# Chunks 0 and 1: gelu as one ScalarE activation, both convolved ahead of the first joint

## The chip, the cores and the metric

One core of one Trainium2 chip. Times are microseconds of device time for the whole kernel; several runs are given, and one further execution was recorded by the hardware profiler. Engines are called as the profile calls them: PE (TensorE), PEld (its weight loads), DVE (VectorE), ACT (ScalarE), POOL (GpSimd), SP (SyncE, which here only issues DMAs).

## The reference

A small speech transducer head, forward and backward. `x` is 2 x 16000 x 256, two strided convolutions with gelu reduce it to 4000 time steps, and a joint with 8 label vectors is formed by tanh:

```python
h = _gelu(conv3(x, w1))[:, ::2, :]          # conv3: three taps, 256 -> 256 channels
f = _gelu(conv3(h, w2))[:, ::2, :]          # _gelu: the tanh approximation
fe = jnp.einsum("btd,de->bte", f, w_f)
ge = jnp.einsum("bud,de->bue", g, w_g)
j = jnp.tanh(fe[:, :, None, :] + ge[:, None, :, :])
out = jnp.einsum("btud,dv->btuv", j, w_o)
# returned: out and the gradients of x, w1, w2, g, w_f, w_g, w_o for a given grad_out
```

All tensors are bf16. The largest are `out` and `grad_out` (2 x 4000 x 8 x 256, 32.8 MB each) and `x` and its gradient (16.4 MB each).

## The kernel before

The 8016 columns of time (both batches, with a gap of 16) are cut into 16 chunks of 512 (`CW`); the last is shorter. Channels lie on partitions, in two halves (`KT`). For each chunk n the kernel goes through these steps, each a Python generator that yields after a unit of work:

- `load_x(n)` brings the four phases of x (every fourth row) transposed into SBUF, one tile `XC` each, from a pool of six. `load_got` and `load_go` bring `grad_out` transposed and straight. All these are DMAs on SP's queue.
- `conv_units(n)` is the first convolution: for each parity of h two halves of six matmuls (L313), ACT copies each out of PSUM (L316), and `gelu` turns them into h (`HT`) and the derivative (`G1`).
- `conv2_units(n)` is the second convolution (L348, L351), with the same gelu giving f (`FT`) and its derivative (`G2`). `fe_units(n)` multiplies by w_f (L372) and copies to `FE` (L374).
- `tanh(n, u)` forms the joint's tanh for label u (`JT`, L389).
- `joint_units(n, up)` does two labels: `gj` squares JT (`JSQ`, L610), multiplies grad_out by w_o transposed (L616) and forms the gradient `NGZ` (DVE, L620); `ngfe_acc` sums NGZ over the labels on POOL (`ACCN`, last into `NGFE`, L639); JT is turned to rows (`JR`; by TensorE in `jr_block` for chunk 0, by DMA in `load_jr` after); the output is formed (L683) and copied (`OUT`, L685); `gwo` accumulates w_o's gradient (L722).
- the backward half of chunk n-1 runs inside chunk n's joint: `d1_units`, `d5_units`, `row_units`, `gwf_units`, `gw2_units`, `ghr_units`, `e_units` (L573 and L586), the last with the rows of x (`XR`) that `load_xr` brings on POOL's queue.

`gelu` is built from Square, a fused add and multiply, Sigmoid and a product (the list `first`), then five DVE operations for the derivative (the list `second`). Chunk 0 does this in halves of 512 columns.

Order: before the chunk loop, a `chain` writes out chunk 0's start: 16 dummy matmuls (`warm`, L766), the small products with g, both convolutions of chunk 0 with all weight transposes between them (`transposed_units`, L797), further dummies, and fe. Then for each chunk `weave` takes a unit of the joint, and after a share of them (`ratio`) a unit of the `fill`, which holds the convolutions of chunk n+1 and the backward half of chunk n-1. Deferred gelu operations wait in two queues, `later` (two per unit) and `late` (one per unit, while `late_open` is set). The order in which an engine gets its instructions is settled afterwards by a scheduler, which goes by this written order and by when inputs are ready; `keep_in_program_order` ties an instruction behind the one written before it on the same engine.

Of the kernel before, what the change touches and what calls it, by code (L numbers as in the profile page):

```python
# [32 lines left out]
def kernel(  # L33
# [173 lines left out]
    def load_xr(n):  # L207
        pin = tc.keep_in_program_order
        load = lambda **kw: pin(nc.gpsimd.dma_start(**kw))
# [29 lines left out]
    def scratch(name, spare):  # L239
        if spare:  # L240
            return rowp.tile([P, 8, P], BF16, name="rows")[:].rearrange("p (k a) b -> p k (a b)", k=KT)
        return gel.tile([P, KT, CW], BF16, name=name)
# [20 lines left out]
    def gelu(xb, W, h, gp, off, kts=((0, KT),), spare=False):  # L263

        sq, s = scratch("g_sq", spare), scratch("g_s", spare)
        TT, TS, STT = nc.vector.tensor_tensor, nc.vector.tensor_scalar, nc.vector.scalar_tensor_tensor
        first, second = [], []
        for (k0, k1) in kts:
            sq_, s_, x_ = sq[:, k0:k1, :W], s[:, k0:k1, :W], xb[:, k0:k1, :W]
            h_, gp_ = h[:, k0:k1, off:off + W], gp[:, k0:k1, off:off + W]  # L270
            first += [
                partial(nc.scalar.activation, out=sq_, in_=x_, func=ACT.Square, scale=GELU_R),
                partial(STT, out=s_, in0=sq_, scalar=1.0, in1=x_, op0=ALU.add, op1=ALU.mult),
                partial(nc.scalar.activation, out=s_, in_=s_, func=ACT.Sigmoid, scale=GELU_A),
                partial(TT, out=h_, in0=s_, in1=x_, op=ALU.mult),
            ]
            second += [
                partial(TS, out=sq_, in0=sq_, scalar1=3.0 * GELU_A, scalar2=GELU_A, op0=ALU.mult, op1=ALU.add),
                partial(TS, out=x_, in0=s_, scalar1=-1.0, scalar2=1.0, op0=ALU.mult, op1=ALU.add),
                partial(TT, out=sq_, in0=sq_, in1=x_, op=ALU.mult),  # L280
                partial(TT, out=sq_, in0=sq_, in1=h_, op=ALU.mult),
                partial(TT, out=gp_, in0=sq_, in1=s_, op=ALU.add),
            ]
        return first, second


    HALVES = ((0, 1), (1, 2))

    seconds0 = []

    def conv_units(n):
# [13 lines left out]
        taps = {0: ((1, 0, 0), (2, 1, 0), (0, 3, -1)), 1: ((0, 1, 0), (2, 3, 0), (1, 2, 0))}  # L305
        for par in range(2):
            xb = gel.tile([P, KT, CW], BF16, name="g_x")
            for mt in range(KT):
# [7 lines left out]
                nc.scalar.copy(out=xb[:, mt, :W], in_=ps[:, :W])  # L316
                yield
            first, second = gelu(xb, W, HT[:, par], G1[:, par], 2, HALVES if n == 0 else ((0, KT),))
            if par == 1 and n > 1:
# [4 lines left out]
            if n == 0:  # L324
                pump(len(first))
        seconds0.extend(seconds)
        if n > 0:
            seconds0.append(lambda: nc.gpsimd.tensor_copy(out=G1[:, 1, :, 1:2],
                                                          in_=S[n - 1]["G1"][:, 1, :, CW + 1:CW + 2]))

    def conv2_units(n):
# [3 lines left out]
        if n > 0:  # L335
            pump(len(later))
# [5 lines left out]
        xb = scratch("g_x", n == 0)  # L342
        for mt in range(KT):
# [7 lines left out]
            nc.scalar.copy(out=xb[:, mt, :W], in_=ps[:, :W])  # L351
            yield
        first, second = gelu(xb, W, FT, G2, 0, HALVES if n == 0 else ((0, KT),), n == 0)
        if n == 0:
            for f in first:
                f()
        else:
            later.extend(first)
# [4 lines left out]
    def fe_units(n):  # L363
        c0, W = geom(n)
        if n > 0:
            pump(len(later))
# [258 lines left out]
    def ngfe_acc(n, u):  # L625
# [13 lines left out]
        nc.gpsimd.tensor_tensor(out=out, in0=in0, in1=st["NGZ", u][:, :, :W], op=ALU.add)  # L639
# [18 lines left out]
    def jr_block(n, up, k):  # L658
        o, M = blocks(geom(n)[1])[k]
        srcs = [(S[n]["JT", 2 * up + j][:, kt, o:o + M], 2 * j + kt, M) for j in range(2) for kt in range(KT)]  # L660
        transposes(srcs, [(S[n]["JR", up][:M, :, :, k].rearrange("p u k d -> p (u k) d"), M, 0, 4)])

    def joint_units(n, up):
# [93 lines left out]
    nc.vector.memset(idle[:], 0.0)  # L757
    small = const.tile([P, 1], FP32, name="small")
    nc.vector.memset(small[:], 0.0)
    nc.scalar.activation(out=small[:], in_=small[:], func=ACT.Sigmoid)  # L760

    def warm(k):

        ps = ps_f32()
        for _ in range(k):
            tc.keep_in_program_order(nc.tensor.matmul(ps[:], lhsT=idle[:, 0, 0:P], rhs=idle[:, 0, 0:CW],  # L766
# [48 lines left out]
    load_jr(0, 0)  # L815

    for n in range(G):
        back, fwd = n > 0, n + 1 < G
        conv = conv_units(n + 1) if fwd else iter(())
        conv2 = conv2_units(n + 1) if fwd else iter(())  # L820
        late_open[0] = False
# [9 lines left out]
        else:  # L831
            parts += [conv, empty(3), islice(conv2, 1), empty(3), conv2, empty(3), fe_units(n + 1)]
        fill = chain(*parts)
        ratio = (0.92 if n > 0 else 0.4) if n + 1 < G else 0.72
        for up in range(U // 2):
# [8 lines left out]
            if up == 1:  # L844
                load_fr(n)
            main = joint_units(n, up)
# [92 lines left out]
```

## Time and profile before

| | us |
|---|---|
| median of 3 runs | 850.12 (849.65 to 863.76) |
| profiled execution | 860.22 |
| its span in the trace | 858.4 |
| PE busy in the span | 816.7 (95%) |
| ACT busy | 678.2 (79%) |
| DVE busy | 621.1 (72%) |
| POOL busy | 372.1 (43%) |
| granted TensorE clock, mean | 0.992 |

How to read it: the busy times are of the whole span. Lines of the profile name a line of the kernel, the engine, the operation and the tiles written and read; in the chain and the timeline the first number is the start in us from the span's start, the second the duration in us, and a bracket behind tells the idle time before and what ended it. Of a group of several instructions in one row (x20) the second number covers all of them. In the windows each row is a stretch of time, with the busy us of each engine, the granted clock, the DMA engines' share and GB/s.

### The profile page before, as it was taken

The numbers are of one execution on the slowest core, as the hardware profiler recorded it, in microseconds if no ns is written. First come the engines' busy times: TensorE is split into PE (matmuls) and PEld (weight loads), VectorE is DVE, ScalarE is ACT, GpSimd is POOL, SyncE is SP. The second block draws the span as 40 slices with busy tenths as digits, with TensorE's granted clock in tenths as the row PEclk, the third lists the DMA queues.
The fourth block names the chain that finished last, engine by engine and source line by source line (L and its number), as shares of the span: only waits on it lengthen the run. The fifth ranks groups of instructions, "written<-read, shape, count | busy, mean of one in ns | idle before, by whom it ended". The sixth has DMA issues, their size and how long they took to land.

```text
span 858.4 us, 16990 instructions
## 1 busy us (share of the span) xinstructions
PE 816.7 (95%) x6396; PEld 598.8 (70%) x6396; DVE 621.1 (72%) x1217; ACT 678.2 (79%) x1080; POOL 372.1 (43%) x367
## 2 busy tenths in 40 slices
PE   6979999999999999899999889999998899999997
PEld 2555676767668676677767667676685676868786
DVE  2997596776869677596876758768696666867745
ACT  2798998796979969699796787969799497896744
POOL 2144453344435434444565534444344243544661
PEclk8999999999999999999999999999999999999999
DMA  9986989999999999999999999999999999998965
GB/s 216 192 191 176 184 207 241 211 250 231 228 211 242 249 209 232 234 232 212 224 209 211 220 226 229 271 199 292 219 235 138 215 267 247 190 267 158 253 167 135
DMA packets 395474, 187.20 MB, mean 218 GB/s; under 512 B 345450, under 2 KB 381186, under 8 KB 393478
## 3 DMA queue, kind: packets, MB, share of 16 engines
q1 hardware_dynamic: 378112, 119.00, 77.5%
q0 software_dynamic: 17280, 67.12, 25.7%
q8 instruction: 50, 0.82, 0.4%
q14 instruction: 32, 0.26, 0.1%
HBM read 51.38 MB, written 50.34 MB: 119 GB/s over the span
## 4 chain that ended last, share of the span: by engine, by line
ACT 42%; PE 37%; DMA 9%; issue 5%; DVE 5%; POOL 0%; SPq 0%; ACTq 0%; POOLq 0%
ACT JT L389 13%; DMA JR<-JT 8%; ACT OUT L685 7%; ACT JSQ L610 6%; PE ps L586 6%; PE GWO_ps L722 5%; PE ps L573 5%; ACT rows L455 4%; PE ps L683 4%; PE ps L348 4%; PE ps L517 4%; PE ps L616 3%; ACT g_s L253 3%; ACT GX L576 3%; ACT g_x L316 2%
## 5 line engine op out<-in xcount | busy, mean ns | idle before, releaser
L639 POOL TENSOR_TENSOR ACCN<-ACCN,NGZ 128x1024 f32<-128x1024 f32 (+1 forms) x80 | 168.7, 2109 | 78.6 <-DVE NGZ L620 76.1
L620 DVE SCALAR_TENSOR_TENSOR NGZ<-JSQ,ps 128x512 bf16<-128x512 bf16 (+3 forms) x272 | 167.4, 640 | 46.2 <-PE ps L616 44.6
L685 ACT CAST OUT<-ps 128x512 bf16<-128x512 f32 (+1 forms) x252 | 148.7, 601 | 62.0 <-PE ps L683 61.8
L389 ACT ACTIVATE JT<-FE,GE 128x512 bf16<-128x512 f32 (+3 forms) x272 | 182.4, 713 | 9.5 <-DMA JR<-JT 9.0
L722 PE MATMUL GWO_ps<-GO,JR 128*128 128x256 bf16 (+1 forms) x1008 | 149.9, 273 | 11.0 <-DMA JR<-JT 8.8
L610 ACT ACTIVATE JSQ<-JT 128x1024 bf16<-128x1024 bf16 (+1 forms) x128 | 136.1, 1067 | 25.7 <-DVE NGZ L620 25.7
L683 PE MATMUL ps<-WO,JT 128*128 128x256 bf16 (+1 forms) x1008 | 148.5, 273 | 0.1
L616 PE MATMUL ps<-GOT,WOT 128*128 128x512 bf16 (+1 forms) x512 | 138.3, 374 | 3.2 <-ACT OUT L685 1.6
L710 POOL DMA_DIRECT2D out_dram<-OUT x76 | 55.9, 736 | 194.5 <-ACT OUT L685 182.8
L722 PEld LDWEIGHTS <-JR 128*128 128x128 bf16 (+1 forms) x1008 | 96.6, 98 | 40.1 <-DMA JR<-JT 10.7
L253 DVE SCALAR_TENSOR_TENSOR g_s<-g_sq,g_x 128x1024 bf16<-128x1024 bf16 (+2 forms) x49 | 82.3, 1680 | 54.4 <-ACT g_sq L253 54.4
L683 PEld LDWEIGHTS <-JT 128*128 128x128 bf16 (+1 forms) x1008 | 97.9, 98 | 21.9 <-issue 1.4
L573 PE MATMUL ps<-W1T,GH 128*128 128x256 bf16 (+2 forms) x756 | 100.5, 273 | 0.0
L401 DVE TENSOR_TENSOR ACC<-ACC,ps 128x512 f32<-128x512 f32 x90 | 61.5, 684 | 51.0 <-PE ps L517 35.0
L313 PE MATMUL ps<-XC,W 128*128 128x512 bf16 (+1 forms) x384 | 93.4, 381 | 4.1 <-DMA XC<-in_x_dram 4.1
L573 PEld LDWEIGHTS <-GH 128*128 128x128 bf16 (+2 forms) x756 | 83.4, 116 | 13.0
L586 PE MATMUL ps<-rows,XR 128*128 128x256 bf16 (+1 forms) x756 | 91.6, 275 | 0.0
L576 ACT CAST GX<-ps 128x512 bf16<-128x512 f32 (+2 forms) x126 | 72.3, 587 | 14.3 <-PE ps L573 8.2
L586 PEld LDWEIGHTS <-XR 128*128 128x128 bf16 (+1 forms) x756 | 74.6, 99 | 12.3
L234 POOL DMA_DIRECT2D out_dram<-GX x67 | 37.3, 558 | 88.0 <-ACT GX L576 83.1
L616 PEld LDWEIGHTS <-WOT 128*128 128x128 bf16 x512 | 48.3, 98 | 35.5 <-issue 3.9
L313 PEld LDWEIGHTS <-W 128*128 128x128 bf16 x384 | 37.9, 99 | 43.1 <-issue 7.2
(131 smaller groups left out, 1188.5 us busy)
## 6 DMA issues: line engine op xcount, KB each, us to landing
GO<-in_grad_out_dram SPq DMA_DIRECT2D x56, 512.0 KB, 5.5
out_dram<-OUT POOLq DMA_DIRECT2D x56, 512.0 KB, 5.4
XR<-in_x_dram POOLq DMA_DIRECT2D x13, 1088.0 KB, 8.6
out_dram<-GX POOLq DMA_DIRECT2D x55, 256.0 KB, 4.3
GOT<-in_grad_out_dram SPq DMA_TRANSPOSE x136, 5.3
JR<-JT SPq DMA_TRANSPOSE x128, 4.7
GO<-in_grad_out_dram SPq DMA_DIRECT2D x4, 384.0 KB, 4.0
out_dram<-OUT POOLq DMA_DIRECT2D x4, 384.0 KB, 4.7
```

What stands on the lines that cost most here:

```text
L253: later.popleft()()
L313: nc.tensor.matmul(ps[:, :W], lhsT=W1[:, i, kt, mt * P:(mt + 1) * P], rhs=st["X", c][:, kt, 16 + sh:16 + sh + W], start=(k == 0), stop=(k ...
L389: nc.scalar.activation(out=JT[:, mt, lo:hi], in_=S[n]["FE"][:, mt, lo:hi], func=ACT.Tanh, bias=GE[:, b, mt, u:u + 1], scale=1.0)
L573: nc.tensor.matmul(ps[:M, cj * D:(cj + 1) * D], lhsT=GH[:, par, kt, o:o + s * (M - 1) + 1:s], rhs=W1T[:, i, kt, :], start=(j == 0), stop=( ...
L586: nc.tensor.matmul(ps[:, dt * D:(dt + 1) * D], lhsT=XR[:M, 4 * k + i + 2 * (1 - par), dt * P:(dt + 1) * P], rhs=t[:M, g + 2 * par:g + 2 * ...
L610: nc.scalar.activation(out=JSQ[:, :, :W], in_=JT[:, :, :W], func=ACT.Square)
L616: nc.tensor.matmul(ps[:, :W], lhsT=WOT[:, kt, mt * P:(mt + 1) * P], rhs=GOT[:, kt, :W], start=(kt == 0), stop=(kt == KT - 1))
L620: nc.vector.scalar_tensor_tensor(out=NGZ[:, mt, lo:hi], in0=JSQ[:, mt, lo:hi], scalar=1.0, in1=ps[:, lo:hi], op0=ALU.subtract, op1=ALU.mul ...
L639: nc.gpsimd.tensor_tensor(out=out, in0=in0, in1=st["NGZ", u][:, :, :W], op=ALU.add)
L683: nc.tensor.matmul(ps[:M, j * V:(j + 1) * V], lhsT=st["JT", u][:, kt, o:o + M], rhs=WO[:, kt, :], start=(kt == 0), stop=(kt == KT - 1))
L685: nc.scalar.copy(out=OUT[:M, k, :], in_=ps[:M, :])
L722: nc.tensor.matmul(GWO_ps[:, dt, :], lhsT=JR[:M, j, dt, k, :], rhs=GO[:M, k, j * V:(j + 1) * V], start=(n_gwo[0] == 0), stop=(n_gwo[0] == ...
```

## The change

For chunks 0 and 1 ACT's `Gelu_apprx_tanh` reads PSUM and writes HT or FT at once; a DVE copy keeps the convolution's result for the derivative in a tile borrowed from the pools of GH (`XS`) or GF. The derivative recomputes Square, the inner term and Sigmoid from that copy, and its eight operations go into lists `deriv[n]` that are put into `late` at the start of chunk n's joint (opened in its third pass for chunk 0, from the beginning for chunk 1). Chunk 1's first convolution stands in the opening chain, two of its units ahead of chunk 0's second convolution; its second convolution follows the first tanh. Eight of nine weight transposes move into chunk 0's joint. Two of the three sets of dummies are dropped. x of chunk 1 is loaded ahead of grad_out; WO, W2 and WF load on POOL's queue; the x rows of chunk 0 are tied behind the last accumulation of chunk 0's joint. JR of chunk 0 is evicted for two blocks at a time.

```diff
-    def load_x(n):
+    def load_x(n, phases=(0, 1, 3, 2)):
-        for c in (1, 0, 3, 2):
+        for c in phases:
...
     def load_xr(n):
-        pin = tc.keep_in_program_order
-        load = lambda **kw: pin(nc.gpsimd.dma_start(**kw))
+        def load(**kw):
+            dma = tc.keep_in_program_order(nc.gpsimd.dma_start(**kw))
+            if n == 0:
+                tc.add_manual_dep(dma.ins, S[0]["last"].ins.name, NOSYNC, reason="x rows behind the joint")
...
+    def derivative(xb, W, h_, gp_):
+        TT, TS, STT = nc.vector.tensor_tensor, nc.vector.tensor_scalar, nc.vector.scalar_tensor_tensor
+        x_, t = xb[:, :, :W], {}
+        def square():
+            t["sq"] = gel.tile([P, KT, CW], BF16, name="g_sq")[:, :, :W]
+            nc.scalar.activation(out=t["sq"], in_=x_, func=ACT.Square, scale=GELU_R)
+        def inner():
+            t["s"] = gel.tile([P, KT, CW], BF16, name="g_s")[:, :, :W]
+            STT(out=t["s"], in0=t["sq"], scalar=1.0, in1=x_, op0=ALU.add, op1=ALU.mult)
+        return [
+            square,
+            inner,
+            lambda: nc.scalar.activation(out=t["s"], in_=t["s"], func=ACT.Sigmoid, scale=GELU_A),
+            lambda: TS(out=t["sq"], in0=t["sq"], scalar1=3.0 * GELU_A, scalar2=GELU_A, op0=ALU.mult, op1=ALU.add),
+            lambda: TS(out=x_, in0=t["s"], scalar1=-1.0, scalar2=1.0, op0=ALU.mult, op1=ALU.add),
+            lambda: TT(out=t["sq"], in0=t["sq"], in1=x_, op=ALU.mult),
+            lambda: TT(out=t["sq"], in0=t["sq"], in1=h_, op=ALU.mult),
+            lambda: TT(out=gp_, in0=t["sq"], in1=t["s"], op=ALU.add),
+        ]
+    deriv = {0: [], 1: []}
...
     def conv_units(n):
+        XS = ghp.tile([P, 2, KT, CW + 4], BF16, name="GH") if n <= 1 else None
-            xb = gel.tile([P, KT, CW], BF16, name="g_x")
+            xb = gel.tile([P, KT, CW], BF16, name="g_x") if n > 1 else XS[:, par]
...
-                nc.scalar.copy(out=xb[:, mt, :W], in_=ps[:, :W])
+                if n <= 1:
+                    nc.scalar.activation(out=HT[:, par, mt, 2:2 + W], in_=ps[:, :W], func=ACT.Gelu_apprx_tanh)
+                    nc.vector.tensor_copy(out=xb[:, mt, :W], in_=ps[:, :W])
+                else:
+                    nc.scalar.copy(out=xb[:, mt, :W], in_=ps[:, :W])
                 yield
+            if n <= 1:
+                deriv[n] += derivative(xb, W, HT[:, par, :, 2:2 + W], G1[:, par, :, 2:2 + W])
+                continue
...
     def conv2_units(n):
-        xb = scratch("g_x", n == 0)
+        xb = gfp.tile([P, KT, CW + 4], BF16, name="GF") if n <= 1 else scratch("g_x")
...
+            if n <= 1:
+                nc.scalar.activation(out=FT[:, mt, :W], in_=ps[:, :W], func=ACT.Gelu_apprx_tanh)
+                nc.vector.tensor_copy(out=xb[:, mt, :W], in_=ps[:, :W])
...
+        if n <= 1:
+            deriv[n][:0] = derivative(xb, W, FT[:, :, :W], G2[:, :, :W])
+            return
...
-        nc.gpsimd.tensor_tensor(out=out, in0=in0, in1=st["NGZ", u][:, :, :W], op=ALU.add)
+        st["last"] = nc.gpsimd.tensor_tensor(out=out, in0=in0, in1=st["NGZ", u][:, :, :W], op=ALU.add)
...
-            for k in range(len(bl)):
-                jr_block(n, up, k)
+            for k in (0, 2):
+                jr_blocks(n, up, k)          # eight transposes, one copy of 1024 columns
...
-    nc.sync.dma_start(out=W2[:], in_=w2.rearrange("i (kt p) n -> p i kt n", p=P))
-    nc.sync.dma_start(out=WF[:], in_=w_f.rearrange("(kt p) n -> p kt n", p=P))
-    nc.sync.dma_start(out=WO[:], in_=w_o.rearrange("(kt p) n -> p kt n", p=P))
-    idle = xcp.tile([P, KT, CW + 16], BF16, name="XC")
+    nc.gpsimd.dma_start(out=WO[:], in_=w_o.rearrange("(kt p) n -> p kt n", p=P))
+    nc.gpsimd.dma_start(out=W2[:], in_=w2.rearrange("i (kt p) n -> p i kt n", p=P))
+    nc.gpsimd.dma_start(out=WF[:], in_=w_f.rearrange("(kt p) n -> p kt n", p=P))
+    idle = rowp.tile([P, 8, P], BF16, name="rows")[:].rearrange("p a b -> p (a b)")
...
-    nc.scalar.activation(out=small[:], in_=small[:], func=ACT.Sigmoid)
+    nc.scalar.activation(out=small[:], in_=small[:], func=ACT.Gelu_apprx_tanh)
...
+    load_x(1, (0, 1, 3))
     for i in range(2):
         load_got(*order[i])
+    load_x(1, (2,))
     load_go(*orderp[0])
     for i in range(2, 4):
         load_got(*order[i])
-    if G > 1:
-        load_x(1)
-    for _ in chain(warm(16), small_units(), conv_units(0), transposed_units(), warm(8), conv2_units(0), warm(20), fe_units(0)):
+    conv1, turned = conv_units(1), transposed_units()
+    for _ in chain(warm(16), small_units(), conv_units(0), islice(turned, 1), islice(conv1, 2), conv2_units(0),
+                   conv1, fe_units(0)):
         pass
...
     load_jr(0, 0)
+    for _ in conv2_units(1):
+        pass
...
-        late_open[0] = False
+        late_open[0] = n == 1
+        if n <= 1:
+            late.extend(deriv[n])
...
-            parts += [conv, empty(3), islice(conv2, 1), empty(3), conv2, empty(3), fe_units(n + 1)]
+            parts += [turned, empty(12), fe_units(1)]
...
+            if n == 0 and up == 2:
+                late_open[0] = True
```

More of the change, by code (lines that the diff above doesn't have):

```diff
@@ L261, in pinned, with gelu @@
         return op if n <= 1 else (lambda: tc.keep_in_program_order(op()))
-    def gelu(xb, W, h, gp, off, kts=((0, KT),), spare=False):
-        sq, s = scratch("g_sq", spare), scratch("g_s", spare)
+    def gelu(xb, W, h, gp, off):
+        sq_, s_, x_ = scratch("g_sq")[:, :, :W], scratch("g_s")[:, :, :W], xb[:, :, :W]
+        h_, gp_ = h[:, :, off:off + W], gp[:, :, off:off + W]
         TT, TS, STT = nc.vector.tensor_tensor, nc.vector.tensor_scalar, nc.vector.scalar_tensor_tensor
[L267 to L283, printed above, removed]
-        return first, second
@@ L287 @@
-    HALVES = ((0, 1), (1, 2))
+        first = [
+            partial(nc.scalar.activation, out=sq_, in_=x_, func=ACT.Square, scale=GELU_R),
+            partial(STT, out=s_, in0=sq_, scalar=1.0, in1=x_, op0=ALU.add, op1=ALU.mult),
+            partial(nc.scalar.activation, out=s_, in_=s_, func=ACT.Sigmoid, scale=GELU_A),
+            partial(TT, out=h_, in0=s_, in1=x_, op=ALU.mult),
+        ]
+        second = [
+            partial(TS, out=sq_, in0=sq_, scalar1=3.0 * GELU_A, scalar2=GELU_A, op0=ALU.mult, op1=ALU.add),
+            partial(TS, out=x_, in0=s_, scalar1=-1.0, scalar2=1.0, op0=ALU.mult, op1=ALU.add),
+            partial(TT, out=sq_, in0=sq_, in1=x_, op=ALU.mult),
+            partial(TT, out=sq_, in0=sq_, in1=h_, op=ALU.mult),
+            partial(TT, out=gp_, in0=sq_, in1=s_, op=ALU.add),
+        ]
@@ L350, in conv2_units @@
                     k += 1
-            nc.scalar.copy(out=xb[:, mt, :W], in_=ps[:, :W])
-            yield
[L353 to L358, printed above, removed]
+            if n <= 1:
+                nc.scalar.activation(out=FT[:, mt, :W], in_=ps[:, :W], func=ACT.Gelu_apprx_tanh)
+                nc.vector.tensor_copy(out=xb[:, mt, :W], in_=ps[:, :W])
+            else:
+                nc.scalar.copy(out=xb[:, mt, :W], in_=ps[:, :W])
+            yield
+        if n <= 1:
+            deriv[n][:0] = derivative(xb, W, FT[:, :, :W], G2[:, :, :W])
+            return
+        first, second = gelu(xb, W, FT, G2, 0)
+        later.extend(first)
         late.extend(pinned(f, n) for f in second + seconds0)
@@ L364, in fe_units @@
         c0, W = geom(n)
-        if n > 0:
-            pump(len(later))
+        pump(len(later))
         FE = fep.tile([P, KT, CW], FP32, name="FE")
```

36 lines of the change are left out of this document (18 added, 18 removed).

## The prediction

> **What bounds the kernel now.** I read the page's slices first (PE 8 to 9 tenths nearly everywhere, 6 and 7 in the first and third), then the windows, which put numbers on that.
>
> ```profile
> core 0: us, PE busy (x) PEld busy (x) DVE busy (x) ACT busy (x) POOL busy (x), PEclk, DMA share, GB/s
> 33.00:77.00 44.00, 37.64 (x264) 23.31 (x263) 37.89 (x79) 40.08 (x62) 19.11 (x13) 0.96 0.79 175
> 77.00:127.00 50.00, 49.29 (x391) 36.53 (x390) 39.09 (x70) 45.84 (x73) 21.06 (x20) 1.00 0.92 200
> 127.00:177.00 50.00, 49.33 (x392) 36.69 (x391) 37.57 (x69) 41.64 (x66) 22.17 (x20) 1.00 1.10 233
> ```
>
> From 77 us on TensorE is busy 49.3 of 50 us: nothing in the change touches those fourteen chunks, so only what precedes can be won. The accumulation's last step per chunk (POOL L639 writing NGFE) marks the chunks:
>
> ```profile
> 74.26 2.13 POOL L639 TENSOR_TENSOR NGFE<-ACCN,NGZ 128x1024 bf16<-128x1024 f32 x1
> 122.97 2.45 POOL L639 TENSOR_TENSOR NGFE<-ACCN,NGZ 128x1024 bf16<-128x1024 f32 x1 [1.03 <-DVE NGZ L620]
> 173.75 2.45 POOL L639 TENSOR_TENSOR NGFE<-ACCN,NGZ 128x1024 bf16<-128x1024 f32 x1 [1.03 <-DVE NGZ L620]
> ```
>
> So 76.4 us pass until chunk 0's joint is summed; then a chunk takes 50.8. The sum is about these 76.4 us. Their chain:
>
> ```profile
> 3.49 10.62 DMA XC<-in_x_dram
> 14.16 3.59 PE ps L313 x8
> ...
> 23.91 1.89 PE ps L766 x8
> 25.80 2.61 PE ps L348 x12
> 28.40 4.32 PE ps L766 x20
> 33.19 1.07 ACT FE L374 x2
> 34.26 2.45 ACT JT L389 x4
> ...
> 37.69 2.52 DVE NGZ L620 x8
> ```
>
> A load of x until 14.1 us, the first convolution, then a stretch in which the chain passes through 28 dummy matmuls (L766), which only fill the time the gelu steps of chunk 0 take. The first NGZ stands at 37.7. From the timeline:
>
> ```profile
> 0.74 1.28 ACT L760 ACT_TABLE_LOAD   x1 [0.74 <-PEq L923]
> 4.77 1.07 POOL L209 DMA_DIRECT2D XR<-in_x_dram  x2
> 14.16 6.61 PE L313 MATMUL ps<-XC,W 128*128 128x512 bf16 x20 [4.08 <-DMA XC<-in_x_dram]
> 17.21 0.29 DVE L258 TENSOR_SCALAR g_sq<-g_sq 128x512 bf16<-128x512 bf16 x1
> 45.35 0.43 DVE L258 TENSOR_SCALAR g_x<-g_s 128x1024 bf16<-128x1024 bf16 x1
> 53.94 2.35 DVE L258 TENSOR_SCALAR g_x<-g_s 128x1024 bf16<-128x1024 bf16 x1
> ```
>
> Two things to see. Twenty matmuls take 6.61 us where 12 take 2.61 later (0.217 each, so 4.3): the windows give a granted clock of 0.50 from 12 to 18 us, after the wait. And the written order is not the executed one: XR belongs to chunk 1's code and the derivative at 17.21 to chunk 0's joint, yet both run far ahead of it. The scheduler fills idle engines with whatever is ready.
>
> **The change, step by step.**
>
> *Loading x.* XR (1,080 KB by the issue view) leaves the first 14 us; WO, W2 and WF (640 KB) take its place on POOL's queue, from SP's, where they stood behind x. SP loses three issues (0.58, 0.53, 4.82), gains x of chunk 1 ahead of GOT and GO. The third x part landed at 14.1 together with about 1.6 MB of POOL's queue since 2.3 (0.135 MB per us) against 0.79 MB of x. At those rates the new 1.19 MB of POOL end at 11.1 with 0.58 MB of x in; the last 0.2 MB at the 0.2 MB/us of later windows take 1 us: 12.1 us. Bounds: 10.3 us (all 1.97 MB at the windows' rates) and 14.1 (if the transposes set their own pace). TensorE then waits 2 us instead of 4.08; of the 2.3 us lost to the clock I save 1.3 (bounds 0 and 2.3). The convolution ends at about 17.4 instead of 20.8.
>
> *Convolving chunk 1 ahead.* Between that end and FE's first copy lie 12.4 us now. Then: four transposes 0.2, and 12+12+12+4 matmuls by 0.217, 8.7. These hide the gelu steps, as the dummies did. x of chunk 1 has two free buffers out of six; its third part waits in SP's queue until chunk 0's first half is convolved (about 15), and lands 4.2 later (median of L164), at 19 to 20, when TensorE arrives at 18.5: wait 1 us (bounds 0 and 4; behind it in SP's queue are GOT and GO, which now land some 12 us before use). FE's copy at about 27.3 instead of 33.2: **-5.9**.
>
> *Gelu in one step.* ACT's GELU reading PSUM is not in the trace. Nearest rows: CAST of the same shape from PSUM 0.58, tanh 0.71. I take 0.58, so it costs what the copy did, and Square, the fused step, Sigmoid and the product (0.63, 0.69, 0.63, 0.42 per half) go off the path. In exchange 12 copies PSUM to SBUF on DVE, 0.69 each by L443: 8.3 us, against the products saved, 6 x 0.42 and 3 x 0.69, 4.6. In the first 20 us DVE works 3.5, so it hides them; without that cover 3.7.
>
> *Tables.* Now one load serves Sigmoid and Tanh. GELU asks for a further one, and the first Sigmoid for a switch. The derivatives' six Sigmoids are written late, but may be pulled forward as L258 was; each one between two GELUs costs two loads, 2.56. Bounds: one load, hidden, and six pairs, 15.4. I take three pairs, 7.7 us, of which ACT's idle time (busy 4.8 of the first 20 us and 7 of the next 13, by the windows) hides all but **+2.2**, the two GELUs of chunk 1's second convolution ahead of JSQ among it. The rule that speaks against the change is here. "Batch activation calls by set, not by function", says the Trainium skill (ScalarE: Activation LUTs, "Table sets: the hidden batching unit"), and its "What ACT_TABLE_LOAD costs" gives an estimate of 2.66 us a switch with its drain; the row's 1.28 shows the load alone, no run here shows the drain, and by 2.66 the three pairs would be 16 us.
>
> The first NGZ follows FE by 4.5 us as now; the first joint's start moves from 37.7 to about 34: **-3.7**.
>
> *Chunk 0's joint* (37.7 to 76.4). It loses 36 matmuls of chunk 1 (7.8 us) and six copies on ACT (3.5), gets 32 weight transposes (1.7) with eight copies on DVE (2.7) and JR evictions in pairs (eight of 0.61 for sixteen of 0.34, by back-to-back starts). But ACT is busy 40 of 44 us and DVE 38, so TensorE's relief is worth nothing itself. What counts: ACT 3.5 less, and a wait that goes. Now fe of chunk 1 waits for FT in the middle of this joint, behind a stretched DVE operation (2.35 where the same took 0.43, under a POOL accumulation); TensorE's gaps of 2.13, 1.56 and 1.48 us and its halved clock (0.89 between 55 and 70) stem from there. With FT done before, I take **-4**. Bounds: +2 (three late derivatives of chunk 0 join those of chunk 1: ACT 5.8, DVE 11) and -11 (ACT's bare work with no derivative in it: tanh, JSQ and OUT of four passes, 6.3 each, and two GELUs or FE copies twice 1.2).
>
> *Chunk 1's joint.* Its derivatives are written into it: DVE 3 x (1.22+2x0.43+3x0.69), less some overlap at their ends, 11 to 12, ACT 3 x 1.92 = 5.8, beside 39 and 46 of 50. Since ready work is pulled ahead, I take **0**; left in place it is +2 to +5, as ACT would need 51.6 of 50 us. XR now comes on POOL's queue after the last accumulation, as in all other chunks; it lands in 8.6 us, some 20 before gw1 (L586) asks for it, and POOL's stores stand behind only its issue of 0.55.
>
> *Rest.* The idle tile and the buffers of GH and GF lent for x wait for no one before chunk 1; POOL's memsets of them no longer run at 5.8 but in POOL's free half. 0.
>
> Sum: -3.7 - 4 + 0 = **-7.7 us**. The profiled execution took 860.2 (span 858.4 and 1.8 around it), so 852.5 by its own time. Its spacing of NGFE shows gaps of 53.7, 53.9, 55.2 and 58.4 where others are 50.8, where the chain waits for JR transposes; the runs shown have a median 10 us lower. The median is the base of the forecast: 850.1 - 7.7 = **842.4**.
>
> **Rivals.**
>
> 1. *More is won.* No Sigmoid falls between GELUs (start -5.9), and the joint comes near ACT's bare work, -9: -15, **835**. For: in the first 33 us ACT is idle 21, room for all 11.6 us of Squares and Sigmoids. Against: DVE stretched by POOL stays.
>
> 2. *Slower: tables thrash.* All six Sigmoids stand alone among GELUs while TensorE waits for ACT: 15.4 us on the path. With -5.9 and -4 that is +5.5, and the half clock after each wait costs about 1.5 more: **857**. It decides from four pairs on the path (4 x 2.56 = 10.2 against 9.9). For: L258 at 17.21. Against: ACT has gaps in the start, and a late GELU of chunk 1 is not asked for at once. By the Trainium skill's 2.66 (same page, same section), as an estimate, it would be 873.
>
> 3. *Derivatives stay where written.* Chunk 1 becomes ACT's, +5: **847**. For: three scratch buffers for six sets of them. Against: L258 again.
>
> 4. *XR was not what held x.* The third part still lands at 14: 3.5 of the start come back, and the wait for chunk 1's third part grows by 0.4: **846.3**. For: the fourth transpose's issue already took 2.87 instead of 1.28, so SP's queue alone is backed up at 7 us. Against: XR ends at 14.3, with x. The Trainium skill (DMA: Bandwidth & Descriptors, "Queues, rings and completion order") says each engine goes round the queues packet by packet; by that x is held by whatever POOL has queued, weights as much as XR; with half of the step's 3.4 lost it would be 844, an estimate.
>
> **How the numbers follow.** Forecast 0.42, rivals 0.18, 0.12, 0.15, 0.13. The range runs from rival 1 and somewhat beyond, for stalls of JR that the median may hold fewer of, 831, to 853, short of rival 2. A measurement of this kernel can tell about 2%, 17 us: faster needs 833 or less, beyond rival 1's own value, so half of that and a little of the forecast, 0.13; slower needs 867, a part of rival 2 with the dearer switch, 0.05; the rest, 0.82, is within 2%.
>
> **What would show it.** Right: L313's wait on XC about 2 us and its end near 17; FE's first copy near 27; first NGZ near 34; NGFE of chunk 0 near 68.5 and the next 48.7 to 51 later; some seven ACT_TABLE_LOAD. Wrong: XC still landing at 14 (rival 4); a dozen loads and TensorE waiting for HT or FT (rival 2); NGFE 0 to NGFE 1 over 53 (rival 3); NGFE 0 before 62 (rival 1); or a difference that arises after chunk 2, which no step here has.

## Result and profile after

| | before | after |
|---|---|---|
| median, us (4 runs each) | 855.80 (849.65 to 863.76) | 879.76 (875.03 to 884.98) |
| ratio of after to before | | 1.0289, 95% interval 1.0226 to 1.0351 |
| profiled execution, its span, us | 860.22, 858.4 | 875.03, 873.3 |
| granted TensorE clock, mean | 0.992 | 0.979 |
| DVE busy, ACT busy, us | 621.1, 678.2 | 622.8, 679.4 |
| first NGZ, us | 37.7 | 45.5 |
| last accumulation of chunk 0 starts | 74.3 | 74.7 |
| last accumulation of chunk 1 starts | 123.0 | 136.2 |

The kernel became slower by some 24 us, where 7.7 us less had been forecast. No engine has more to do: DVE and ACT are busy for practically as long as before. A ratio leaves out runs more than 1.5% above their kernel's fastest, whereas medians are of all runs; in chunks from 2 on, waits for JR transposes come and go from run to run in both kernels, so profiles are compared only up to chunk 1's last accumulation.

The loss is there at that point already: the two profiled spans differ by 14.9 us, and 13.3 of it have arisen by then. First the rows of the last accumulation, from the timeline of POOL after:

```profile
74.66 3.00 POOL L666 TENSOR_TENSOR NGFE<-ACCN,NGZ 128x1024 bf16<-128x1024 f32 x1
136.22 2.45 POOL L666 TENSOR_TENSOR NGFE<-ACCN,NGZ 128x1024 bf16<-128x1024 f32 x1 [1.04 <-DVE NGZ L647]
187.23 2.45 POOL L666 TENSOR_TENSOR NGFE<-ACCN,NGZ 128x1024 bf16<-128x1024 f32 x1 [1.03 <-DVE NGZ L647]
```

From 74.66 to 136.22 chunk 1 takes 61.6 us; before, it took 48.7. The next chunk takes 51.0, against 50.8. So there are two things to explain: an opening that ends 7.8 us later although it was to be shorter, and a chunk 1 that is 12.9 us longer. Between them chunk 0's joint gains: from its first NGZ to the end of its last accumulation it takes 32.1 us (45.5 to 77.7) instead of 38.7.

**The opening.** The same stretch of the timeline as was shown of before, now after:

```profile
0.74 1.28 ACT L791 ACT_TABLE_LOAD   x1 [0.74 <-PEq L962]
10.16 1.87 PE L334 MATMUL ps<-XC,W 128*128 128x512 bf16 x4
12.94 6.46 PE L334 MATMUL ps<-XC,W 128*128 128x512 bf16 x20 [0.91 <-DMA XC<-in_x_dram]
13.98 0.60 ACT L338 ACTIVATE HT<-ps 128x512 bf16<-128x512 f32 x1 [11.75 <-PE ps L334]
14.62 0.69 DVE L339 CAST GH<-ps 128x512 bf16<-128x512 f32 x1 [4.10 <-ACT HT L338]
30.31 3.57 PE L334 MATMUL ps<-XC,W 128*128 128x512 bf16 x8 [9.82 <-DMA XC<-in_x_dram]
45.52 0.68 DVE L647 SCALAR_TENSOR_TENSOR NGZ<-JSQ,ps 128x512 bf16<-128x512 bf16 x1
58.90 1.28 ACT L300 ACT_TABLE_LOAD   x1
```

Chunk 0's convolution now waits only 0.91 us, and ends at 19.4. But then four matmuls of chunk 1's convolution run, and TensorE stands for 9.82 us: the third part of chunk 1's x isn't there until 30.3. The eight matmuls behind this wait take 3.57 us, 0.45 each, where 12 took 2.61 (0.22 each). SP's queue, from its timeline, shows why x is late:

```profile
0.75 13.35 SPq L164 DMA_TRANSPOSE XC<-in_x_dram  x6
14.14 2.65 SPq L172 DMA_TRANSPOSE GOT<-in_grad_out_dram  x2
16.83 0.58 SPq L198 DMA_DIRECT2D GO<-in_grad_out_dram  x1
17.47 5.57 SPq L172 DMA_TRANSPOSE GOT<-in_grad_out_dram  x3
23.09 1.13 SPq L198 DMA_DIRECT2D GO<-in_grad_out_dram  x2
24.33 9.10 SPq L164 DMA_TRANSPOSE XC<-in_x_dram  x5
```

The second column is the time in which the queue was busy issuing. The source has the third part of x ahead of every GOT and GO. In the queue five GOT and three GO stand ahead of it: it could not start until chunk 0's convolution had freed a buffer, the others could, and so the scheduler put them first. They took the queue from 14.1 to 24.2 us. When x had its buffer, it was behind them.

**Chunk 1.** The windows, first of before and then of after (us, then busy us of each engine, the granted clock, DMA share, GB/s):

```profile
60.00:78.00 18.00, 14.38 (x97) 9.03 (x95) 13.91 (x30) 15.14 (x24) 10.85 (x6) 0.91 0.53 147
78.00:90.00 12.00, 12.00 (x93) 7.77 (x91) 8.43 (x15) 11.53 (x18) 3.08 (x3) 1.00 1.05 200
90.00:102.00 12.00, 11.29 (x100) 8.55 (x98) 7.54 (x16) 12.00 (x19) 4.58 (x4) 1.00 0.81 188
102.00:114.00 12.00, 12.00 (x100) 9.51 (x98) 9.68 (x17) 8.34 (x14) 6.65 (x6) 1.00 0.91 196
```

```profile
core 0: us, PE busy (x) PEld busy (x) DVE busy (x) ACT busy (x) POOL busy (x), PEclk, DMA share, GB/s
60.00:78.00 18.00, 15.35 (x106) 10.37 (x104) 17.20 (x27) 15.54 (x24) 9.61 (x7) 0.91 0.81 184
78.00:90.00 12.00, 9.96 (x77) 6.39 (x76) 11.90 (x20) 10.82 (x16) 4.34 (x7) 1.00 0.95 219
90.00:102.00 12.00, 7.63 (x51) 4.06 (x48) 11.84 (x23) 11.54 (x16) 1.48 (x3) 1.00 1.20 242
102.00:114.00 12.00, 9.69 (x69) 7.31 (x70) 6.47 (x12) 7.28 (x12) 4.97 (x4) 0.72 0.45 93
```

From 60 to 102 us DVE is now busy 40.9 of 42 us (17.20 + 11.90 + 11.84); before, it was 29.9. ACT, the other engine that the derivatives use, is no busier than it was (37.9 us, before 38.7). So DVE is the bound there, and TensorE starves: from 78 to 114 it is idle 8.7 of 36 us where it was idle 0.7, and in the last of these stretches it has a clock of 0.72. That costs by estimate another 2.2 us (0.28 of 12, less half of the 2.3 us in which it stood idle there). Together (8.7 - 0.7 + 2.2) that is about 10.2 of the 12.9 us. What DVE does more of is the derivatives: their rows take 24.6 of its 40.9 us from 60 to 102; before, L258 took 4.2 of 29.9. Three rows of DVE, one of POOL, two of ACT and two of TensorE after:

```profile
61.39 2.25 DVE L302 TENSOR_SCALAR GF<-g_s 128x1024 bf16<-128x1024 bf16 x1
84.88 2.35 DVE L302 TENSOR_SCALAR GF<-g_s 128x1024 bf16<-128x1024 bf16 x1
114.80 0.68 DVE L305 TENSOR_TENSOR G<-g_sq,g_s 128x1024 bf16<-128x1024 bf16 x1
...
84.77 2.17 POOL L666 TENSOR_TENSOR ACCN<-NGZ 128x1024 f32<-128x1024 bf16 x1 [4.05 <-DVE NGZ L647]
...
95.49 1.07 ACT L300 ACTIVATE g_s<-g_s 128x1024 bf16<-128x1024 bf16 x1
96.44 2.56 ACT L416 ACTIVATE JT<-FE,GE 128x512 bf16<-128x512 f32 x4
...
87.88 0.38 PE L467 MATMUL ps<-GF,W2T 128*128 128x512 bf16 x1 [1.39 <-DVE GF L446]
104.31 0.61 PE L753 MATMUL GWO_ps<-GO,JR 128*128 128x256 bf16 x2 [4.97 <-DMA JR<-JT]
```

The derivative rows stretch from 61.4 to 115.5 us, three sets of chunk 0 up to 80 and three of chunk 1 from 82. An operation that takes 0.42 us alone takes 2.25 and 2.35 beside a POOL accumulation. TensorE's longest wait, 4.97 us, is for a transposed JR: ACT forms the JT for it at 96.4, right behind the Sigmoid of a derivative (95.5). Before, chunk 0's derivatives ran between 17 and 36 us, in the opening, where their 9.3 us of DVE fitted beside 8.1 of its other work. After, only a Square (38.0), a fused step (39.1) and one further operation (41.5) ran that early.

### The profile page after: what moved, and what is told of

Same layout as the page of the kernel before. It is cut to its first block, busy times and chain, and to the rows that moved or that the text cites. A ratio compares the mean times of both kernels' runs of the same rounds, so it can differ in the third digit from the quotient of the medians.

```text
span 873.3 us, 16905 instructions
## 1 busy us (share of the span) xinstructions
PE 819.4 (94%) x6368; PEld 599.0 (69%) x6368; DVE 622.8 (71%) x1194; ACT 679.4 (78%) x1075; POOL 374.4 (43%) x370
## 4 chain that ended last, share of the span: by engine, by line
ACT 41%; PE 36%; DMA 8%; DVE 6%; issue 6%; SPq 3%; POOL 0%; ACTq 0%; POOLq 0%
ACT JT L416 13%; ACT OUT L716 7%; ACT JSQ L637 6%; DMA JR<-JT 6%; PE ps L613 6%; PE GWO_ps L753 5%; PE ps L600 5%; PE ps L714 5%; PE ps L544 4%; ACT rows L482 4%; PE ps L373 4%; PE ps L643 3%; ACT g_s L254 3%; ACT GX L603 3%; ACT g_x L341 2%
## 5 line engine op out<-in xcount | busy, mean ns | idle before, releaser
L716 ACT CAST OUT<-ps 128x512 bf16<-128x512 f32 (+1 forms) x252 | 148.8, 601 | 62.7 <-PE ps L714 62.1
L637 ACT ACTIVATE JSQ<-JT 128x1024 bf16<-128x1024 bf16 (+1 forms) x128 | 135.8, 1067 | 24.2 <-DVE NGZ L647 24.2
L714 PE MATMUL ps<-WO,JT 128*128 128x256 bf16 (+1 forms) x1008 | 151.3, 275 | 2.4 <-ACT g_x L341 0.9
L753 PEld LDWEIGHTS <-JR 128*128 128x128 bf16 (+1 forms) x1008 | 97.3, 99 | 40.6 <-DMA JR<-JT 11.0
L254 DVE SCALAR_TENSOR_TENSOR g_s<-g_sq,g_x 128x1024 bf16<-128x1024 bf16 (+1 forms) x42 | 73.1, 1740 | 51.9 <-ACT g_sq L254 51.9
L334 PE MATMUL ps<-XC,W 128*128 128x512 bf16 (+1 forms) x384 | 95.6, 388 | 12.4 <-DMA XC<-in_x_dram 10.7
```

What stands on the lines that cost most here:

```text
L254: later.popleft()()
L334: nc.tensor.matmul(ps[:, :W], lhsT=W1[:, i, kt, mt * P:(mt + 1) * P], rhs=st["X", c][:, kt, 16 + sh:16 + sh + W], start=(k == 0), stop=(k ...
L637: nc.scalar.activation(out=JSQ[:, :, :W], in_=JT[:, :, :W], func=ACT.Square)
L714: nc.tensor.matmul(ps[:M, j * V:(j + 1) * V], lhsT=st["JT", u][:, kt, o:o + M], rhs=WO[:, kt, :], start=(kt == 0), stop=(kt == KT - 1))
L716: nc.scalar.copy(out=OUT[:M, k, :], in_=ps[:M, :])
L753: nc.tensor.matmul(GWO_ps[:, dt, :], lhsT=JR[:M, j, dt, k, :], rhs=GO[:M, k, j * V:(j + 1) * V], start=(n_gwo[0] == 0), stop=(n_gwo[0] == ...
```

## Experiments

My theory after the result: two faults that don't depend on each other, the late third part of x and the late derivatives. The rivals: that the gelu's own operations or the table loads are what costs; that the opening's loads only move the wait elsewhere; and that something lasting comes in behind chunk 2. "Lead" below is how much earlier than in the kernel before (123.0) chunk 1's last accumulation starts; a negative one is later.

**The kernel after once more** (no edit).

> The changed kernel once more, unaltered. Theory (the loss stands in two places before 139 us: TensorE's 9.8 us wait for the third x part of chunk 1, and the derivatives that fill DVE from 60 to 102 us): the last accumulation of chunks 0 and 1 starts again near 74.7 and 136.2 us, within 1 us, and the later chunks differ only by chance waits for JR transposes. Rival (a lasting change of the transposes' order on SP's queue): the last two chunks again take some 87 us from one last accumulation to the next but one, where the kernel before took 80.

877.69 us against 859.47, ratio 1.0207 (1.0138 to 1.0277). First NGZ 46.2, chunk 1 66.5 us, lead -18.3. The wait for x is 8.43 us. Both faults are there again, at sizes that vary by 1 to 5 us: chunk 0 came as expected, chunk 1 by 5 us later than expected. From 90 to 110 us TensorE waits 9.6 us for JR transposes in three waits, where after had the one of 4.97, and DVE is busy 37.0 of the 42 us from 60 to 102. So the share of JR in the second fault varies. The loss at chunk 1 (13.3 and 18.3) and in the total (24 and 18.2) are of similar size.

**Opening loads kept in their written order.**

```diff
 # load_got and load_go, while the opening is written
-            nc.sync.dma_start_transpose(out=t[:, :, col:col + w], in_=grad_out[b, q:q + w, u, :])
+            dma = nc.sync.dma_start_transpose(...)
+            if opening[0]:
+                tc.keep_in_program_order(dma)
```

> The loads of grad_out in the opening are tied to the written order on SP's queue, so the third x part of chunk 1 goes ahead of them. Theory: it lands near 20 us instead of 30.3, TensorE's wait shrinks from 9.8 to under 2 us, the first NGZ moves from 45.5 to about 36, the last accumulation of chunk 0 from 74.7 to about 66, and chunk 1 still takes 61: some 9 us faster than the changed kernel, 868 to 871. Rival (the bytes, not the order: 4.9 MB are asked for before the first joint, 24 us at 0.2 MB per us): the x part or the first GOT lands late all the same, chunk 0 ends at 72 or later, and the time stays within 3 us.

```profile
14.05 6.67 PE L340 MATMUL ps<-XC,W 128*128 128x512 bf16 x20 [2.95 <-DMA XC<-in_x_dram]
37.59 0.38 PE L834 MATMUL pst<-ident,W 128*128 128x128 bf16 x4 [0.21 <-ACT OUT L722]
49.36 1.89 PE L649 MATMUL ps<-GOT,WOT 128*128 128x512 bf16 x4 [2.32 <-DMA GOT<-in_grad_out_dram]
```

These are all the waits that TensorE's timeline marks between 12 and 60 us. The wait for the third part has gone; the first NGZ comes at 35.0 instead of 45.5 and chunk 0's accumulation at 65.0. A GOT comes 2.32 us late in exchange. The order of SP's queue was the cause of the late opening. The forecast had 34 for the first NGZ, but the nearness is partly luck: the first convolution ends at 20.7 instead of 17.4, while the table loads that were forecast at 2.2 us don't come there. Chunk 1 is still 62.7 us (lead -4.7), with a wait of 6.32 us for JR: the second fault is on its own. In the total nothing is seen of the 10 us (886.51 against 859.47, ratio 1.0222, 1.0144 to 1.0300). The profiled execution has chunks of 62.0 and 56.7 us and a last one of 53.0 (32.5 and 40.8 in the two profiles of before), with ACT waiting for JR transposes; whether these belong to this kernel or to the runs is open.

**Derivatives of both chunks from the start of chunk 0's joint.**

```diff
-        late_open[0] = n == 1
-        if n <= 1:
-            late.extend(deriv[n])
+        late_open[0] = n == 0
+        if n == 0:
+            late.extend(deriv[0] + deriv[1])
```

> Both chunks' derivatives are queued from the first unit of chunk 0's joint on, none in chunk 1's. Theory: chunk 0's joint gets longer by 4 to 6 us (last accumulation 79 to 81), chunk 1 falls from 61.6 to 49 to 52 us, so the last accumulation of chunk 1 starts near 130 instead of 136: 4 to 7 us faster than the changed kernel. Rival (chunk 1 is held by x of chunk 2 and JR, which stand late on SP's queue, not by DVE): chunk 1 stays at 58 or more.

Chunk 1 is back to 49.1 us and TensorE no longer waits for a JR in it, which shows that its extra 12.9 came from derivatives inside it. But chunk 0's accumulation starts at 86.0 instead of 74.7: DVE is busy 18.00 of 18 us between 60 and 78 and 12.00 of 12 between 78 and 90. The cost has moved into the first joint; lead -12.1, 1.2 us better than after. 869.62 us against 859.47, ratio 1.0111 (1.0056 to 1.0165).

**Both edits together.**

> Loads tied as written and derivatives early. Theory: the two gains add up, first NGZ near 36, last accumulation of chunk 1 near 121 to 123, which is 2 to 4 us ahead of the kernel before (122.97): a time within 1% of before, either way. Rival (either loss only uncovers the other, since derivatives then crowd the joint): chunk 1's last accumulation stays at 128 or later.

First NGZ 33.5, chunk 0 at 74.5, chunk 1 49.1 us, lead -0.6: with both faults treated the kernel is where it was at chunk 1, and what was won in the opening (4.2 us) goes to the derivatives in the first joint. The total isn't: 868.0 against 859.47, ratio 1.0102 (1.0037 to 1.0167), so that by the interval at least 2 us are lost behind chunk 1, for which no run here shows a cause.

**The derivatives' price**, on the kernel with the loads in order.

```diff
 def derivative(xb, W, h_, gp_):
     ...
+    return [lambda: TT(out=gp_, in0=x_, in1=h_, op=ALU.mult)]
```

> Loads tied as in a1_pin, and of each derivative of chunks 0 and 1 only one product on DVE is left, with no Square, fused step, Sigmoid or the other four (the derivative's values are left out). Theory (the derivatives' 22 us on DVE and 11.6 on ACT are what crowds chunk 1): chunk 0's last accumulation near 60 to 63, chunk 1's 49 to 51 after it, so near 111 against 127.7 in a1_pin: 13 to 17 us less. Rival (x of chunk 2 and JR late on SP's queue): chunk 1 stays above 56.

This kernel leaves the derivatives' values out: one product is left of each. Chunk 0 at 56.5, chunk 1 at 108.4: 19.3 us earlier than with the loads in order alone (127.7), 1.0 of it in the opening, 7.5 in the first joint, 10.8 in chunk 1. 840.59 against 863.78, ratio 0.9785 (0.9646 to 0.9924).

```profile
60.00:78.00 18.00, 17.07 (x118) 10.11 (x117) 12.53 (x19) 17.62 (x26) 3.72 (x5) 1.00 1.06 238
78.00:90.00 12.00, 11.53 (x100) 8.71 (x99) 7.84 (x18) 12.00 (x19) 5.32 (x5) 1.00 1.05 221
90.00:102.00 12.00, 12.00 (x104) 10.46 (x103) 9.98 (x16) 10.34 (x18) 6.03 (x6) 1.00 1.03 208
```

In its windows DVE is down to 30.4 of 42 us and TensorE up to 40.6. The derivatives on DVE and ACT, not the gelu step, are what chunk 1 pays for. No run takes away the share of one of the two engines alone; that DVE is the tighter one rests on the windows.

**Derivatives that can run in the opening:** Tanh instead of Sigmoid, and each list in the order in which its inputs appear, with the two edits above.

```diff
-    lambda: nc.scalar.activation(out=t["s"], in_=t["s"], func=ACT.Sigmoid, scale=GELU_A),
+    lambda: nc.scalar.activation(out=t["s"], in_=t["s"], func=ACT.Tanh, scale=0.5 * GELU_A),
+    lambda: TS(out=t["s"], in0=t["s"], scalar1=0.5, scalar2=0.5, op0=ALU.mult, op1=ALU.add),
...
-            deriv[n][:0] = derivative(xb, W, FT[:, :, :W], G2[:, :, :W])
+            deriv[n] += derivative(xb, W, FT[:, :, :W], G2[:, :, :W])
```

> Loads tied; the derivatives' Sigmoid replaced by Tanh with a DVE step to halve and shift it, so that no activation table changes before chunk 2; the two derivatives of the first convolution stand ahead of that of the second, and all are queued from the first joint unit on. Theory (the derivative of the second convolution, first in the list, kept the others from the opening's idle DVE and ACT): two Squares and one derivative run before the first NGZ, chunk 0's last accumulation near 70 to 72 against 74.5 in a3_both, chunk 1 takes 49 to 51, so 120 to 122: 853 to 859, level with before or a little ahead. Rival (DVE and ACT have no room left in the opening): 123 or later, no better than a3_both.

Squares now run at 18.5, 22.5 and 27.7 and the first Tanh of a derivative at 20.9, with no table load until 80.9 (a Sigmoid of chunk 2). Chunk 0 at 69.1, chunk 1 at 119.9, lead 3.1. 860.59 against 863.78, ratio 0.9968 (0.9902 to 1.0033). Where the derivatives stand decides: with the same gelu and the same loads this is 5.4 us ahead of the kernel with both edits at the end of chunk 0, in spite of three DVE operations more for each chunk. Tanh and the list order weren't run apart.

**The kernel before once more** (no edit).

> The kernel before, unaltered, profiled a second time. Theory (the changed kernel's last chunk, 39 to 40 us in both profiles with a 6.2 us wait of ACT for JR in each, is a lasting loss, since the instruction order there is that of before): the last chunk here takes 32 to 34 us again and ACT's waits for JR in it stay under 3 us. Rival (chance: JR transposes land late in either kernel): the last chunk takes 38 or more here too, and the changed kernel's loss lies before chunk 2 alone.

865.84 against 863.78 in the runs beside it. First NGZ 37.9, chunk 0 at 74.5, chunk 1 at 123.2: up to there the profile repeats within 0.3 us. Its last chunk takes 40.8 us, where the first profile of before had 32.5 and after 39.6. So the slower tail that I had seen in after is nothing of the change, and as a lasting loss it falls.

**XR late and nothing else**, on the kernel before.

```diff
 # load_xr, kernel before
+            if n == 0:
+                tc.add_manual_dep(dma.ins, S[0]["last"].ins.name, NOSYNC, reason="x rows behind the joint")
```

> The kernel before with the x rows of chunk 0 tied behind the last accumulation of chunk 0's joint, and nothing else of the change. Theory: the first convolution's wait for the third x part falls from 4.1 us to 2 or 3, the first NGZ moves by 1 to 2 us at most, and the time stays within 0.5% of before. Rival (the DMA engines are the second bound, 187 MB at about 220 GB/s: 1.1 MB moved from the opening into the joint costs its 5 us): last accumulation of chunk 1 the same or earlier, yet 4 to 6 us slower in all, by waits for JR in later chunks.

```profile
9.43 0.24 PE L783 MATMUL ps<-gT,WG 128*128 128x8 bf16 x4 [0.26 <-DVE gT L779]
9.53 5.34 PE L316 MATMUL ps<-XC,W 128*128 128x512 bf16 x24
14.71 0.39 PE L800 MATMUL pst<-ident,WO 128*128 128x128 bf16 x4
```

TensorE's timeline: 24 matmuls in one run with no wait for x, in 5.34 us. The convolution ends at 14.9 instead of 20.8, the first NGZ stands at 32.3, lead 5.3. XR was what held x. In the total this can't be told from nothing: 860.11 against 863.78, ratio 1.0017 (0.9959 to 1.0075). A lead of 5.3 us kept to the end would be a ratio of 0.994, outside the interval, so by these runs part of it is lost behind chunk 1.

**Weights back on SP's queue**, on the kernel after.

```diff
-    nc.gpsimd.dma_start(out=WO[:], ...)      # and W2, WF
+    nc.sync.dma_start(out=WO[:], ...)        # and W2, WF
```

> The changed kernel with WO, W2 and WF back on SP's queue, behind chunk 0's x; nothing else altered. Theory (whatever is in POOL's queue beside the first x delays it, weights as much as the x rows): TensorE no longer waits for the third x part, the clock stays full and the first convolution ends near 15 instead of 19.4, as in b1_xrlate; the wait for chunk 1's third part, still behind grad_out on SP's queue, grows by most of that, so the first NGZ comes at 43 to 45.5 and the time is within 3 us of the changed kernel. Rival (SP's own transposes set the pace): the first convolution ends at 18 to 20 as before.

The first x is waited for no more and chunk 0's convolution ends at 14.2 us, 5.2 us earlier than after. The wait for chunk 1's third part grows from 9.82 to 12.53 (it ends at 28.0), so 2.7 of it are lost at once; first NGZ 44.2, chunk 1 at 137.1. 869.01 against 865.94, ratio 1.0133 (0.9922 to 1.0343). The 640 KB of weights held x on POOL's queue as XR's 1,080 KB had.

**Chunk 0 alone with the one-step gelu**, chunk 1 as in the kernel before, weights on SP's queue, Tanh and list order as above, no dummies behind the transposes.

```diff
-    if n <= 1:      # gelu from PSUM, copies to borrowed tiles, derivative list
+    if n == 0:
...
-    load_x(1, (0, 1, 3))
```

> One part of the change alone, for chunk 0 only: gelu in one step from PSUM, its derivatives by Tanh in the first joint, x rows late, JR in pairs of blocks; chunk 1 is convolved in chunk 0's joint by the old gelu, the weights load on SP's queue and all nine transposes stay in the opening, the dummies behind them go. Theory: no wait for x, first convolution done near 15, FE near 22, first NGZ near 27 against 32.3 in b1_xrlate; the joint carries chunk 0's derivatives beside chunk 1's gelu, so its last accumulation comes at 66 to 69 and chunk 1's near 115 to 117. Rival (DVE, already 38 of 44 us busy in that joint, takes all of it back): chunk 1's last accumulation at 120 or later. In time 0.5 to 1.5% faster than the kernel before by the theory.

```profile
core 0: us, PE busy (x) PEld busy (x) DVE busy (x) ACT busy (x) POOL busy (x), PEclk, DMA share, GB/s
30.00:70.00 40.00, 31.18 (x201) 19.22 (x203) 37.47 (x68) 33.95 (x48) 15.21 (x10) 0.84 0.76 170
```

The first NGZ comes at 32.2, where XR late alone gives 32.3: the one-step gelu brings nothing of its own there. FE's first copy does come 6.6 us earlier (21.2 against 27.8), but then TensorE waits 3.86 us for chunk 1's x, until 28.0, ahead of the matmuls that the first NGZ needs. Then DVE, busy 37.5 of 40 us, takes the rest back; lead 0.2. 861.40 against 865.94, ratio 1.0054 (0.9993 to 1.0116).

**Everything mended:** loads in order, weights on SP's queue and tied there too, both chunks' derivatives early, Tanh and list order.

> As a8_tanh_early (loads tied, Tanh instead of Sigmoid in the derivatives, those of the first convolution first, all queued early), with the three weights back on SP's queue behind chunk 0's x. Theory: another 3 to 4 us off the opening, first NGZ near 31, last accumulation of chunk 1 near 116 against 119.9, so 1% faster than the kernel before. Rival (the later chunks wait the more for JR the sooner TensorE gets there, since 187 MB have to pass): the opening gains and the whole does not, as b1_xrlate, which was 5 us ahead at chunk 1 and level in the end.

First NGZ 29.5, chunk 0 at 63.5, chunk 1 at 114.4, lead 8.6. 855.97 against 865.94, ratio 0.9933 (0.9861 to 1.0006): not quite apart from 1, so it was run again.

> The kernel of c2_all once more, in five rounds. Its first profile had chunk 1's last accumulation at 114.4 us where the kernel before has 123.0 and 123.2 in two profiles. Theory: the lead of 8.6 us is kept to the end, since the instructions after chunk 2 stand in the same order in both, so the total is 8 to 9 us shorter, a ratio of about 0.990, and this profile has chunk 1's last accumulation within 1 us of 114.4. Rival: the lead is given back in the later chunks, because the chip's DMA engines, not the instruction order, bound them; then the totals differ by under 3 us, a ratio of 0.997 to 1.003.

```profile
64.78 2.44 POOL L673 TENSOR_TENSOR NGFE<-ACCN,NGZ 128x1024 bf16<-128x1024 f32 x1 [0.60 <-DVE NGZ L654]
115.62 2.44 POOL L673 TENSOR_TENSOR NGFE<-ACCN,NGZ 128x1024 bf16<-128x1024 f32 x1 [1.03 <-DVE NGZ L654]
```

Lead 7.4, chunk 1 coming 1.2 us later than the first time, just outside what was expected; 851.33 against 863.84, ratio 0.9868 (0.9794 to 0.9941). This version beats the kernel before, by about 1%. Its lead at chunk 1 agrees with the total, where the interval stands for 5 to 18 us; the rival, that the later chunks give it back, doesn't hold for it.

| kernel | first NGZ | chunk 0 | chunk 1 | its length |
|---|---|---|---|---|
| before | 37.7 | 74.3 | 123.0 | 48.7 |
| after | 45.5 | 74.7 | 136.2 | 61.6 |
| loads in order | 35.0 | 65.0 | 127.7 | 62.7 |
| derivatives early | 45.0 | 86.0 | 135.0 | 49.1 |
| both | 33.5 | 74.5 | 123.5 | 49.1 |
| both, Tanh, list order | 34.7 | 69.1 | 119.9 | 50.8 |
| the same, weights on SP | 29.5 | 63.5 | 114.4 | 50.9 |

## Why the prediction was wrong, by its steps

- **Price of gelu and copies: right.** GELU 0.60 (forecast 0.58), copy 0.69 (0.69).
- **Tables: over-sized.** Not three pairs but one load in all, at 58.9, in the middle of the first joint; rival 2 falls. The reason is the one that hurts elsewhere: no Sigmoid went into the opening. By the Trainium skill's advice to batch activations by set (ScalarE: Activation LUTs, "Table sets: the hidden batching unit") the change would have been the worse for its tables; no run here has GELU and Sigmoid in turns, so none shows it.
- **Loading x: right direction, too large.** The wait is 0.91 instead of the forecast 2, but the first four matmuls start 1.1 us later and all 24 run slowly, so the convolution ends at 19.4, not 17.4: 1.4 of the 3.4 us. In the other profiles with the weights on POOL's queue it ends between 19.1 and 20.7, which is at most 1.6 us gained. XR late alone brings 5.9 (14.9), and with the weights taken off POOL's queue the changed kernel ends it 5.2 earlier. The lost part is what the sentence under rival 4 said: by the Trainium skill (DMA: Bandwidth & Descriptors, "Queues, rings and completion order") each engine goes round the queues packet by packet. By that, weights hold x as XR did, and the runs agree: 0.64 MB on that queue cost 5.2 us. Rival 4's own claim, that XR wasn't what held x, is refuted.
- **Convolving chunk 1 ahead: the first failed step.** "Wait 1 us (bounds 0 and 4)" was 9.82, outside both bounds. I had seen that GOT and GO stand near x in SP's queue, and called them "behind it". I used the scheduler's habit of running what is ready for DVE work, but not for DMA issues, although the same rule lets eight loads with free buffers pass one that waits. The landing time in that step, 4.2 us, is 4.5 by the view of L164; it changes nothing. FE's first copy came at 39.95 instead of 27.3, so -5.9 became +6.8, and the first NGZ +7.8 instead of -3.7. With the order tied FE came at 29.5 and the first NGZ at 35.0, 1 us from the forecast, in part because the table loads forecast at 2.2 us stayed away.
- **Chunk 0's joint: right, under-sized.** -4 forecast, -6.6 measured. TensorE's wait for FT in it is gone, and with the loads in order the joint gains the same 6.6 (30.0 us from first NGZ to the start of its last accumulation, before 36.6), so the gain doesn't come from the late start.
- **Chunk 1's joint: the second failed step.** I took 0, with +2 to +5 if the derivatives stay where they were written. They stayed, and it was +12.9 and +17.7. Rival 3 had the mechanism ("NGFE 0 to NGFE 1 over 53": 61.6), but priced it by ACT's sum of 51.6 in 50 us. By the windows DVE was the engine: it is busy 11.1 us more from 60 to 102, ACT 0.8 less. My 11 to 12 us for chunk 1's three sets were 14.1 (82 to 116), and chunk 0's sets, which that sum left out, put 14.6 just ahead of them (60 to 82). I added the 11 to 12 to DVE's 39 of 50 as if they could lie anywhere, while all come in one stretch, some stretched by POOL; then JR transposes come late (4.97 us; 9.6 in the second profile), and behind that wait TensorE has the lower clock (0.72 from 102 to 114). L258 at 17.21, my evidence that derivatives are pulled forward, was of a kernel in which their Sigmoid had run already for the gelu itself. In the changed kernel Square and Sigmoid became part of the derivative, and the list starts with that of the second convolution, ready last.
- **Sum.** Up to chunk 1's last accumulation: +7.8 in the opening, -7.4 from first NGZ to the start of chunk 0's last accumulation (-6.6 to its end), +12.9 in chunk 1, together +13.3 in one profile and +18.3 in the other, where -7.7 was forecast. The ratios, 1.021 and 1.029, stand for 18 to 25 us. On the kernel with its loads in order, leaving out the derivatives gains 19.3 us up to there. The forecast's base of 850.1, a median of three runs, was 5.7 us low by itself: with the fourth run it is 855.8.
- **What stays open.** The kernel with its loads in order loses some 19 us by its ratio with a lead of only -4.7, both edits together some 9 with -0.6, and XR late alone shows nothing of 5.3. The first runs of after lose 24 where the lead is -13.3. So in four of these comparisons, by their intervals, something is lost behind chunk 1 that the two faults don't explain. Waits for JR transposes are large enough to hide or make such differences: they ended 44 us of ACT's idle time in the profile with the loads in order and 24 with XR late, but 9 and 18 in the two of before. What sets them wasn't tried.

## What to carry to other kernels

When an operation is fused away but one of its by-products is still needed, cost the recomputation where it will really run: look for the idle stretch that used to hide it, and ask whether its inputs are ready in that stretch, list order included. A load that must wait for a buffer is passed by every load that needn't, so on a shared DMA queue tie the order if the waiting one is needed first. And price such a step on each engine in the windows where it will lie: DVE at 39 of 50 us on average had no room for 11 us in one stretch.

## What the runs showed of the hardware

- With 0.64 MB of plain loads moved off POOL's queue, the first convolution, which needs the transposed x of SP's queue, ended 5.2 us earlier (19.4 to 14.2), and with 1.08 MB moved off it 5.9 us earlier (20.8 to 14.9).
- After a wait of 9.8 us eight matmuls took 3.57 us, 0.45 each. With no wait from 9.5 us on, 24 took 5.34 (0.22 each).
- One load of the activation tables (1.28 us, at 58.9) served the change from GELU to Sigmoid; GELU, Tanh, Square and copies ran side by side without a further one.
